# Batch 1 of x in one transfer of eight heads on the casting queue, instead of two of four

## The chip, the cores and the metric

The kernel runs on one core of one Trainium2 chip. The metric is device microseconds (us) of one execution; the three runs of the kernel before took 213.36, 213.55 and 213.91 us, median 213.55. The engines are named as the profile names them: PE (TensorE matmul), PEld (its weight loads), DVE (VectorE), ACT (ScalarE), POOL (GpSimd), SP (SyncE). Each has its own instruction stream, executed in order, and waits on semaphores that other engines and transfers raise.

## The reference

Two steps. The first is a cross attention in which, for each of 8 batches and 8 heads, 512 token rows `x` and 32 state rows `state` (64 wide) read each other with the same scores, the softmax taken over the state rows for the one and over the token rows for the other:

```python
scores = scale * np.matmul(x, state.transpose(0, 1, 3, 2))
a = np.exp(scores - scores.max(-1, keepdims=True))
a /= a.sum(-1, keepdims=True) + 1e-09
xread = np.matmul(a, state)                        # tokens read the state
scores2 = scale * np.matmul(state, x.transpose(0, 1, 3, 2))
a2 = np.exp(scores2 - scores2.max(-1, keepdims=True))
a2 /= a2.sum(-1, keepdims=True) + 1e-09
sread = np.matmul(a2, x)                           # the state reads the tokens
attn = np.concatenate([xread, sread], axis=2)      # 8 x 8 x (512 + 32) x 64
```

The second is a gated feed-forward layer over the 4352 rows of `attn` (8 heads side by side, 512 wide):

```python
gate = 1.0 / (1.0 + np.exp(-(x @ w_gate)))         # 512 -> 1536
out = gate * (x @ w_val) @ w_out                   # 1536 -> 512, float32
```

## The kernel before, in words

Nothing is scheduled by a planner: the instructions of each engine stand in the order in which the kernel's body calls its helpers, one flat list of calls from L563 on for the start and batches 0 to 2, then `step(b, f)` for the rest. The framework only adds the semaphore waits that the data need.

For a batch `b` the work goes: load x (tile `xf`, 128 partitions x 8 heads x 4 rows x 64), cast it to bfloat16, transpose it on PE into `xT`, multiply by the state (`Sp`), exponential on ACT (`E`), row sums and reciprocals on DVE (`rsq`, `riq`), normalize (`ab`), transpose on PE (`aTp`, copied to `aT`). The attention read is folded into the first layer: `state @ w` is formed once per batch (`swp`, copied to `SW`), and `gvp` = `SW` x `aT` gives gate and value at once. `rdp` is the read of the tokens by the state. The output product uses a seven-product scheme over halves of the matrices (`outp`).

The lines that the change touches belong to the first 14 us.

- **x of batch 0** comes as float32 in four transfers of two heads, all issued by SP (`load_xp`, L87), and is cast on ACT or DVE (`cast_xp`, L95). Its scores are done in quarters: `Sq_mm`, `Sq_exp`, `nq_sum`, `nq_mul`, one for each two heads.
- **x of batch 1** comes through the queue of POOL, which can cast on the way, so it lands as bfloat16 (`load_xh`, L100): heads 0 to 3 in one transfer, heads 4 to 7 in another. On the same queue stand, in order, the weights in pieces (`load_w`, L104) and the state (`load_sb`, L527). Every transfer on this queue gets the next of eight completion semaphores, DMASW0 to DMASW7, in turn; the one that comes ninth waits for the first, and so on.
- **PE** transposes heads 0 to 3 of batch 1 in `xT_mm(1, 0, S0, 2)` (8 transposes, L132) and heads 4 to 7 in `xT_mm(1, 2, S1, 2)`. Between the two stand on PE `Sq_mm(0, 3)` (scores of heads 6 and 7 of batch 0, L174) and `warm(3, G0)` (three matmuls on a tile of zeros, L517).

The calls in that piece, in the order of the list (`load_x...` and `nq_...` calls between them left out): `xT_mm(0, 3, S3)`, `xT_mm(1, 0, S0, 2)`, `Sq_mm(0, 3, OU)`, `warm(3, G0)`, `xT_mm(1, 2, S1, 2)`, `S_mm(1, 0, OU)`, `aT_mm(0, AT)`. On ACT: `xT_cp(0, 3)`, `Sq_exp(0, 1)`, `Sq_exp(0, 3)`, `xT_cp(1, 0)`, `S_exp(1, 0)`, `aT_cp(0, 0)`. On DVE: `nq_sum` of quarters 2, 0, 1, 3, then `nq_mul` of quarters 3 and 2, then `xT_cp(1, 2)`.

Of the kernel before, what the change touches and what calls it, by code (L numbers as in the profile page):

```python
# [16 lines left out]
def kernel(  # L17
# [71 lines left out]
    def xh_tile(b):  # L89
        if b not in xhs:  # L90
            xhs[b] = stg.tile((128, H, 4, D), BF, name="xf", padded_shape=(128, 2 * H, 4, D))

    def cast_xp(b, cp, lo, n):
        xh_tile(b)
        cp(xhs[b][:, lo:lo + n], xfs[b][:, lo:lo + n])  # L95

    def load_xh(b, lo, n):
        xh_tile(b)
        v = x[b].rearrange("h (p c) d -> p h c d", c=4)
        nc.gpsimd.dma_start(xhs[b][:, lo:lo + n], v[:, lo:lo + n])  # L100
# [9 lines left out]
    def zero(t, eng):  # L110
        (nc.gpsimd if eng is pool else nc.vector).memset(t, 0.0)
# [455 lines left out]
    zero(sbz, pool)  # L567
    warm(4, S1)
    make_identity(nc, ident)
    load_xh(1, 0, 4)  # L570
    nc.vector.memset(ones, 1.0)
    cast_s(0, vec)
    cast_xp(0, act, 0, 2)
    load_xh(1, 4, 4)
    zero(sTd, vec)
    sT_mm(0, S1)
    load_xp(0, nc.sync, 4, 2)
# [459 lines left out]
```

## Time and profile before

| | |
|---|---|
| runs | 213.36, 213.55, 213.91 us; median 213.55 |
| span of the profiled execution | 212.3 us, first to last instruction |
| median less that span | 1.25 us around it |
| PE busy | 204.3 us, 96% of the span |
| DVE, ACT, POOL busy | 76%, 61%, 37% |
| granted TensorE clock | 0.997 over the span |

The profile is of one execution. The page has the busy time of each engine, the span in 40 slices, and the chain of work that ended last: followed back from the last instruction, at each step to what released it. A row of the timeline reads: start, duration, engine, line, operation, output<-input, shape, count, and in brackets how long the engine sat idle before it and what released it. For a transfer, the last number is the time from its issue to its landing; a time window given with that view selects the issues that lie in it. The size of a transfer is that on the chip, so x of batch 1 counts 256 KB for four heads in bfloat16. In the rows of the DMA queues, q1 is the queue of SP, q10 that of ACT and q0 that of POOL.

### The profile page before, as it was taken

How to read it: one execution, taken by the hardware profiler on the slowest of the kernel's cores; microseconds unless marked ns; L12 is line 12 of the kernel's file. 1: busy time of each engine (PE TensorE's matmuls, PEld its weight loads, DVE VectorE, ACT ScalarE, POOL GpSimd, SP SyncE). 2: the span in 40 equal slices, each digit the busy share in tenths (PEclk: the TensorE clock that was granted, in tenths of full speed). 3: DMA queues.
4: the chain of work that ended last, by engine and by line, in shares of the span. 5: the costliest groups of instructions: out<-in, count | busy, mean ns of one | idle time of the engine just before them, and what ended most of it. 6: DMA issues, size and time to landing. Idle time of an engine off the chain costs nothing.

```text
span 212.3 us, 5333 instructions
## 1 busy us (share of the span) xinstructions
PE 204.3 (96%) x2089; PEld 132.9 (63%) x2089; DVE 160.3 (76%) x308; ACT 129.6 (61%) x244; POOL 78.1 (37%) x103
## 2 busy tenths in 40 slices
PE   7779999999999999999999999999999999999991
PEld 2545443677666666575666566657566666788981
DVE  2598899998987788578866887688748876865681
ACT  3878898754767477856786578647764663333210
POOL 8799458599042705900491029201500000000000
PEclk9999999999999999999999999999999999999998
DMA  6999999662589943996822621273110400221133
GB/s 205 163 192 191 214 289 183 119 212 40 78 224 333 136 91 110 302 94 208 249 42 48 173 99 28 58 120 153 29 31 35 166 2 0 99 102 49 39 112 99
DMA packets 41320, 27.14 MB, mean 128 GB/s; under 512 B 23632, under 2 KB 39248, under 8 KB 41296
## 3 DMA queue, kind: packets, MB, share of 16 engines
q1 hardware_dynamic: 31088, 20.00, 36.9%
q0 software_dynamic: 9776, 6.49, 19.8%
q10 hardware_dynamic: 432, 0.33, 0.6%
q8 instruction: 16, 0.26, 0.5%
q14 instruction: 8, 0.07, 0.1%
HBM read 18.35 MB, written 8.91 MB: 128 GB/s over the span
## 4 chain that ended last, share of the span: by engine, by line
PE 91%; DMA 3%; DVE 2%; ACT 1%; SPq 1%; issue 0%
PE gvp L355 30%; PE outp L425 29%; PE gvp L343 10%; PE gvp L358 5%; PE outp L442 4%; PE swp L286 4%; DMA xf<-in_x_dram 3%; PE swp L293 2%; PE outp L484 2%; PE Sp L147 1%; PE outp L467 1%; PE rdp L262 1%; SPq L87 1%; DVE rsq L186 1%; PE aTp L234 1%; PE rdp L265 1%
## 5 line engine op out<-in xcount | busy, mean ns | idle before, releaser
L369 DVE SCALAR_TENSOR_TENSOR glu<-th,gvp 128x512 bf16<-128x512 f32 (+1 forms) x108 | 70.1, 655 | 36.7 <-PE gvp L355 13.7
L364 ACT ACTIVATE th<-gvp 128x512 f32<-128x512 f32 (+1 forms) x108 | 62.1, 578 | 49.3 <-PE gvp L355 34.8
L355 PE MATMUL gvp<-aT,SW 128*128 128x512 bf16 x288 | 77.4, 379 | 0.1
L329 ACT CAST SW<-swp 128x512 bf16<-128x512 f32 x83 | 46.5, 592 | 9.3 <-PE swp L286 8.3
L425 PEld LDWEIGHTS <-Sm 128*128 128x128 bf16 x324 | 31.7, 98 | 12.6
L355 PEld LDWEIGHTS <-SW 128*128 128x128 bf16 x288 | 26.7, 98 | 17.3 <-issue 3.6
L200 POOL CAST Eb<-E 128x256 bf16<-128x256 f32 x32 | 12.8, 438 | 52.0 <-ACT E L167 52.0
L425 PE MATMUL outp<-tw,Sm 128*128 128x256 bf16 x240 | 31.8, 273 | 0.0
L425 PEld LDWEIGHTS <-glu 128*128 128x128 bf16 x240 | 23.5, 98 | 10.2
L425 PE MATMUL outp<-wo,glu 128*128 128x256 bf16 x168 | 22.9, 273 | 0.0
L343 PE MATMUL gvp<-aT,SW 128*128 128x512 bf16 x96 | 22.6, 379 | 0.0
L227 POOL TENSOR_TENSOR ab<-E,ri 128x512 bf16<-128x512 f32 x13 | 14.3, 1100 | 11.8 <-DVE ri L210 7.1
L407 DVE TENSOR_TENSOR Sm<-glu 128x768 bf16<-128x768 bf16 (+1 forms) x34 | 18.0, 535 | 0.0
L433 DVE SCALAR_TENSOR_TENSOR res<-outp,U 128x512 f32<-128x512 f32 x22 | 15.0, 685 | 1.2 <-PE outp L442 0.9
L343 PEld LDWEIGHTS <-SW 128*128 128x128 bf16 x96 | 8.6, 97 | 10.4 <-issue 1.8
L116 POOL CAST xb<-xf 128x1024 bf16<-128x1024 f32 x12 | 13.2, 1128 | 1.9 <-DMA xf<-in_x_dram 1.9
L358 PE MATMUL gvp<-xb,wgv 128*128 128x256 bf16 x96 | 12.6, 272 | 0.0
L167 ACT ACTIVATE E<-Sp 128x512 f32<-128x512 f32 x14 | 8.4, 599 | 6.7 <-PE Sp L147 5.7
L425 PE MATMUL outp<-wo,Sm 128*128 128x256 bf16 x84 | 11.5, 273 | 0.0
L358 PEld LDWEIGHTS <-wgv 128*128 128x128 bf16 x96 | 9.3, 98 | 1.3
L251 POOL CAST xs<-xf 128x1024 bf16<-128x1024 f32 x10 | 10.2, 1044 | 0.0
L425 PE MATMUL outp<-tw,glu 128*128 128x256 bf16 x72 | 9.8, 273 | 0.0
(105 smaller groups left out, 213.3 us busy)
## 6 DMA issues: line engine op xcount, KB each, us to landing
out_dram<-res SPq DMA_DIRECT2D x14, 512.0 KB, 3.4
xf<-in_x_dram SPq DMA_DIRECT2D x5, 1024.0 KB, 7.5
wo<-in_moe_w_out_dram POOLq DMA_DIRECT2D x3, 512.0 KB, 7.8
xf<-in_x_dram SPq DMA_DIRECT2D x4, 256.0 KB, 3.9
wgv<-in_moe_w_gate_dram POOLq DMA_DIRECT2D x4, 256.0 KB, 7.7
wgv<-in_moe_w_val_dram POOLq DMA_DIRECT2D x4, 256.0 KB, 8.8
xf<-in_x_dram POOLq DMA_DIRECT2D x1, 1024.0 KB, 9.5
out_dram<-res SPq DMA_DIRECT2D x3, 256.0 KB, 2.2
```

The source lines that it names most:

```text
L116: cp(xbs[b].rearrange("p c h d -> p h c d")[:, lo:lo + n], (xhs if b in xhs else xfs)[b][:, lo:lo + n])
L200: nc.gpsimd.tensor_copy(Ebs[b][:, c], E1s[b][:, c])
L227: (nc.gpsimd if eng is pool else nc.vector).tensor_tensor(half(b, i, abs_), e1, ri.unsqueeze(len(ri.shape)).to_broadcast(e1.shape), ALU.mult)
L329: cp(*sw_left.pop((b, lo, w, e)))
L343: nc.tensor.matmul(ps, SWs[b][:, g, w, fs], aTs[b][:, :, g], start=(g == 0), stop=(g == 1))
L355: nc.tensor.matmul(ps, SWs[b][:, g, w, fs], aTs[b][:, :, g], start=(g == 0), stop=(g == 1))
L358: nc.tensor.matmul(ps, (wg, wv)[w][:, j, fs], held["XS"][:, j], start=(j == 0), stop=(j == 3))
L364: nc.scalar.activation(th, held["gv", b, f][0], AF.Tanh, scale=0.5)
L369: nc.vector.scalar_tensor_tensor(glus[b][:, f], held["th", b, f], 1.0, held["gv", b, f][1], ALU.add, ALU.mult)
L407: eng.tensor_tensor(S_(b, t)[:, i], a, c, op)
L425: nc.tensor.matmul(wps[key][:, c], lhs[:, i, c * 128:(c + 1) * 128], rhs[:, i], start=(first and c == 0 and i == 0), stop=(i == NF // 2 - ...
L433: nc.vector.scalar_tensor_tensor(to, wps[key], 0.5, held["w", name], ALU.mult, ALU.add)
```

## The change

One call loads all eight heads at the place where the first four were loaded; the second call is gone.

```diff
     make_identity(nc, ident)
-    load_xh(1, 0, 4)
+    load_xh(1, 0, 8)
     nc.vector.memset(ones, 1.0)
     cast_s(0, vec)
     cast_xp(0, act, 0, 2)
-    load_xh(1, 4, 4)
     zero(sTd, vec)
```

On POOL, at the start of its list of transfers, two rows become one with twice the rows of data:

```order
 masks.py:199 ISA
 masks.py:199 AFFINE_SELECT ident<-ident 128x128 [waits Pool_49]
-L100 DMA xf<-in_x_dram 128x4x256 x2
+L100 DMA xf<-in_x_dram 128x8x256
 L104 DMA wgv<-in_moe_w_gate_dram 128x4x256
 L104 DMA wgv<-in_moe_w_val_dram 128x4x256
```

Everything behind it on POOL stands in the same order, and each transfer's completion semaphore has a number one lower.

On PE, at `xT_mm(1, 2, S1, 2)` (heads 4 to 7 of batch 1), the wait for the second transfer (DMASW1 before) falls away:

```order
 L517 LDWEIGHTS wm
 L517 MATMUL warm<-wm 128x512
-L132 LDWEIGHTS xf [waits DMASW1_49]
+L132 LDWEIGHTS xf
 L132 MATMUL xTp<-ident,xf 128x128 [waits PE_49]
 L132 LDWEIGHTS xf
```

Twenty-odd rows ahead of it on PE, where the last transpose of batch 0 (tile xf_133) is followed by the first of batch 1 (tile xf_128), the row that waits for DMASW0 stands as it did:

```order
L132 LDWEIGHTS xf_133
L132 MATMUL xTp_194<-ident_96,xf_133 128x128
L132 LDWEIGHTS xf_128 [waits DMASW0_49]
L132 MATMUL xTp_199<-ident_96,xf_128 128x128
L132 LDWEIGHTS xf_128
```

These are the rows of before; in the changed kernel the wait at this place has the same name, but DMASW0 is now raised by the transfer of all eight heads.

## Prediction

> **What bounds the kernel now.** I read the windows view first, because a share over the whole span mixes the start with the rest. Columns: stretch, its length, then busy time (and instructions) of PE, PEld, DVE, ACT and POOL, the granted clock, DMA share, GB/s.
>
> ```profile
> 2.00:8.40 6.40, 5.17 (x39) 2.37 (x36) 2.44 (x6) 3.51 (x7) 6.33 (x11) 1.00 1.01 240
> 8.40:14.00 5.60, 4.32 (x68) 2.79 (x72) 4.99 (x14) 4.39 (x10) 4.50 (x9) 1.00 1.41 187
> 14.00:205.00 191.00, 190.87 (x1960) 124.79 (x1960) 150.47 (x281) 120.86 (x229) 65.81 (x81) 1.00 0.55 124
> ```
>
> From 14 us to 205 us PE is busy for 190.87 of 191 us. So there is nothing in those 191 us that could take up a late start, and nothing that could be shortened by an earlier weight. Whatever moves the moment at which PE gets its backlog, at about 14 us, moves the end by the same amount. Before that PE has holes, and the chain of waits says what sets its pace there (start, length, what):
>
> ```profile
> 2.27 5.45 DMA xf<-in_x_dram
> ...
> 7.74 0.62 ACT xf L95
> 8.36 0.29 ACT E L182
> 8.65 0.03 issue
> 8.68 0.43 DVE rsq L186
> ...
> 10.41 0.29 DVE rsq L186
> ...
> 10.73 0.21 DVE riq L188
> ...
> 10.97 1.06 DVE ab L193 x2
> ...
> 12.17 0.62 PE aTp L234 x8
> ...
> 12.81 1.08 ACT aT L244 x2
> ...
> 13.94 0.42 PE rdp L265 x32
> ```
>
> The last transfer of x of batch 0 lands at 7.72, then ACT casts it, then four reductions and reciprocals follow each other on DVE, one for each quarter of batch 0. The fourth of them, at 10.41, is that of heads 6 and 7. After it come the normalization, the transposes of `ab`, the copies of `aT` and at 13.94 PE's unbroken work. The transfers of batch 1 do not stand in this chain. The question is how far from it they are. The timeline of that piece:
>
> ```profile
> 7.74 0.62 ACT L95 CAST xf<-xf 128x512 bf16<-128x512 f32 x1 [0.34 <-DMA xf<-in_x_dram]
> 8.41 0.23 PEld L132 LDWEIGHTS <-xf 128*128 128x128 bf16 x4 [0.55 <-ACT xf L95]
> 8.81 0.45 PEld L132 LDWEIGHTS <-xf 128*128 128x128 bf16 x8 [0.17 <-DMA xf<-in_x_dram]
> 8.85 0.59 ACT L135 COPY xT<-xTp 128x512 bf16<-128x512 bf16 x1
> 9.33 0.87 ACT L182 ACTIVATE E<-Sp 128x256 f32<-128x256 f32 x2
> 9.48 0.17 PEld L174 LDWEIGHTS <-xT 128*128 128x128 bf16 x4 [0.23 <-ACT xT L135]
> 9.59 0.34 PEld L517 LDWEIGHTS <-wm 128*128 128x128 bf16 x3
> 10.10 1.01 ACT L135 COPY xT<-xTp 128x1024 bf16<-128x1024 bf16 x1
> 10.37 0.45 PEld L132 LDWEIGHTS <-xf 128*128 128x128 bf16 x8 [0.43 <-DMA xf<-in_x_dram]
> ```
>
> The row at 8.81 is `xT_mm(1, 0)`, heads 0 to 3 of batch 1: PE already waits there, 0.17 us, for the first transfer. The row at 10.37 is `xT_mm(1, 2)`, heads 4 to 7: it waits 0.43 us for the second. Between them PE does the scores of heads 6 and 7 of batch 0 (9.48), which feed the second exponential in the ACT row at 9.33 (it ends at 10.20) and through it the fourth reduction of the chain.
>
> **The change part by part.**
>
> *One wait removed.* The wait of 0.43 us at 10.37 goes. Nothing in the chain comes from there: `aT_mm(0)` at 12.17 is released by `ab`, not by batch 1. Worth nothing.
>
> *One issue removed on POOL.* Two issues take 1.68 us together, a later one of eight heads in float32 takes 0.93:
>
> ```profile
> 2.73 1.68 POOL L100 DMA_DIRECT2D xf<-in_x_dram  x2
> 4.39 0.75 POOL L104 DMA_DIRECT2D wgv<-in_moe_w_gate_dram  x1
> 10.02 1.19 POOL L193 TENSOR_TENSOR ab<-E,riq 128x256 bf16<-128x256 f32 x2 [1.10 <-DVE riq L188]
> 11.96 1.42 POOL L200 CAST Eb<-E 128x256 bf16<-128x256 f32 x4
> 21.92 0.93 POOL L82 DMA_DIRECT2D xf<-in_x_dram  x1
> ```
>
> So the six transfers behind it are issued some 0.7 us sooner, and POOL waits longer ahead of its first `ab` at 10.02, where it has 1.10 us idle already. Their landing isn't set by the issue but by the queue, below, so this too is worth nothing. If the weights did come sooner, the PE row of the long window shows that no time is lost to them. If they came later by up to a microsecond, PE would be as late by then.
>
> *One transfer in place of two.* This is the part that costs. The semaphore that `xT_mm(1, 0)` waits for is now raised when all eight heads have landed. PE stands still at 8.81 until then; behind it on PE are the scores of heads 6 and 7, the `warm` matmuls, and all the rest. When does the merged transfer land? The issues, one window for each half and the next (time from issue to landing last), and the packets that the queue of POOL (q0) and of SP (q1) moved in the microseconds from 4 (q1 alone), 5, 6, 7 and 10:
>
> ```profile
> xf<-in_x_dram POOLq DMA_DIRECT2D x1, 256.0 KB, 6.0
> ...
> xf<-in_x_dram POOLq DMA_DIRECT2D x1, 256.0 KB, 6.7
> wgv<-in_moe_w_gate_dram POOLq DMA_DIRECT2D x1, 256.0 KB, 7.3
> ```
>
> ```profile
> q1 hardware_dynamic: 378, 0.36, 106.7%
> ...
> q0 software_dynamic: 155, 0.08, 60.2%
> q1 hardware_dynamic: 183, 0.17, 53.9%
> ...
> q0 software_dynamic: 280, 0.14, 103.3%
> ...
> q0 software_dynamic: 207, 0.10, 80.4%
> ...
> q0 software_dynamic: 394, 0.19, 145.0%
> ```
>
> The first half lands at 2.73 + 6.0 = 8.73, the second at about 10.35 (PE goes on at 10.37), the first piece of weights at 4.39 + 7.3 = 11.7. The steps are 1.6 and 1.35 us for equal sizes: the queue is a stream that works off its bytes in order. Merging doesn't lessen the bytes. Three values for the landing L:
>
> - If the stream's slowest engine is never idle today, L stays at 10.35.
> - If the 0.25 us by which the step between the halves exceeds the next step come from the second issue, they go: 8.73 + 1.35 = 10.1.
> - Lower end: all of the slack in the stream goes. Eight heads are 1024 packets of 512 B (0.51 MB); 155 move from 5 to 6 us beside the tail of batch 0 as today, the other 869 at the 394 per us of the full stream, 2.2 us, so until 8.2. Today the first half's 512th packet moves at 7.4 (155 + 280 by 7, then 77 of 207) and the landing is at 8.73, 1.3 later. That gives L = 9.5.
> - Upper end: no packet moves until all rows of the transfer are described, as late as the second issue ended today, 0.75 us after the first: 10.35 + 0.75 = 11.1.
>
> I take L = 10.2, between the first two, since both rest on the steps of the very rows.
>
> From L to the end: the eight weight loads start 0.05 us after it and take 0.45 us (the rows at 8.81 and 10.37), so the scores of heads 6 and 7 start at L + 0.52 instead of 9.48, a shift of L - 8.96. That step had waited 0.23 us for the ACT copy of `xT` anyway, which is why the shift is less than that of the wait. Their exponential now starts when the scores are done, the same shift, and ends at 10.20 + (L - 8.96). The fourth reduction started at 10.41 because DVE was busy with the third; with its exponential at 10.20 and 0.03 us of hand-over it had 0.18 us to spare. Chain shift: L - 8.96 - 0.18 = L - 9.14. With L = 10.2 that is **1.06 us**, and at 9.14 the cost would begin. The rest of the chain (0.21, 1.06, 0.62, 1.08 us) keeps its lengths. The transposes of heads 0 to 3 are copied on ACT behind the late exponential, then PE does `S_mm(1, 0)`; that follows the exponential's end by 1.0 us for the copy and ends before `aT_mm(0)` at about 13.2, so it adds nothing. POOL's `Eb` copies need the same exponential, which ends at about 11.4, before they start today (11.96).
>
> Sum: -0 (wait) -0 (issue) + 1.06 (PE held). The span of 212.3 becomes 213.4; with the 1.25 us by which the median of the runs exceeds that span, 214.6.
>
> **A rule that speaks for the change.** The Trainium skill, "DMA: Bandwidth & Descriptors", section "Anatomy of one DMA — SWDGE (gpsimd) path", gives a transfer a fixed cost of about 2.0 us and then bytes over 436 GB/s, and its rules for kernel authors say to coalesce. By it an estimate for the merged transfer is 2.0 + 2.4 us for the 1 MB read, after an issue that ends near 3.8: L = 8.2, no wait at all, and the time stays at 213.55. The trace does not agree for transfers that stand behind each other: steps of 1.35 us leave no room for 2.0 us each.
>
> **The rivals.**
>
> *Mostly hidden.* L is near its lower end, 9.5, because the two halves leave a hole: 207 packets from 7 to 8 us against 394 later. For it: that row. Against it: the last landing of a transfer is set by the slowest engine, and the halves' step of 1.6 us is only 0.25 over the later ones, so that engine hardly idles. Shift 0.36 us, 213.9: within what can be told from no change (0.3%, 0.64 us, which L = 9.78 would reach). This is also where the rule above would lead.
>
> *Late start.* L = 11.1, shift 1.96, 215.5. For it: q0 moved nothing before 5 us though its first issue ended at 3.66, so descriptions take time to become packets. Against: eight heads of float32 were issued in 0.93 us at 21.92, no more than 0.2 over a half.
>
> *Faster.* The last transfer of batch 0 shares the engines with q0 from 5 us on (183 packets of q1 beside 155). If the merged transfer starts moving later, batch 0 lands sooner; ACT, which had been idle for 0.34 us ahead of its cast at 7.74, starts the chain up to 0.34 us earlier: 213.2. It decides only if L is also below 9.14 - 0.34 = 8.8, and a transfer that starts later and still has all eight heads down by the time that four take today is hard to see.
>
> **How the numbers follow.** Forecast (L from 9.8 to 10.7) 0.63; mostly hidden 0.17; late start 0.15; faster 0.05. So slower 0.78, same 0.17, faster 0.05. The range 213.7 to 215.4 runs from L = 9.3 to L = 11.0; it leaves out the faster case, the tail of the hidden one and half of the late start.
>
> **What would show it.** Right: PE idle ahead of the `xT_mm(1, 0)` row rises from 0.17 to about 1.6 us with the transfer as releaser; that row starts at 10.2 to 10.3; the transfer's time to landing is about 7.5 us; `aTp` starts at about 13.2; the chain of waits goes from the transfer of batch 1 through the scores and exponential of heads 6 and 7 to the fourth reduction; from 15 us on each row is later by one constant. Wrong: the row starts before 9.2, or starts late while `aTp` still starts at 12.2 (something takes up the delay), or the delay at 14 us is gone by 205 us. The length of the steps after the landing would be wrong if the granted clock fell below 1.00 in this stretch.

## The result, and the profile after

The changed kernel takes 216.89 us (median of four runs, 216.12 to 217.54) against 213.73 for the kernel before in the same comparison (213.36 to 214.42): ratio 1.0127, 95% interval 1.0086 to 1.0169. A second comparison of the same code gave 216.58 against 213.72, ratio 1.0142 (1.0112 to 1.0173). (The quotient of the two medians, 1.0148, lies inside the first interval.) It is slower, as forecast, but by 2.7 to 3.2 us and not by 1.06: above the range of 213.7 to 215.4.

The windows of the changed kernel's profile, in 2 us steps where the pause lies (stretch, its length, busy time and instructions of PE, PEld, DVE, ACT, POOL, then the granted clock, DMA share, GB/s):

```profile
2.00:8.40 6.40, 5.11 (x43) 2.14 (x40) 3.38 (x7) 4.13 (x9) 6.17 (x10) 1.00 1.11 247
8.40:10.00 1.60, 0.00 (x0) 0.00 (x0) 1.21 (x5) 0.59 (x2) 0.72 (x2) 1.00 1.42 189
10.00:12.00 2.00, 0.21 (x3) 0.21 (x4) 0.00 (x0) 0.00 (x0) 1.22 (x2) 0.84 1.45 196
12.00:14.00 2.00, 2.00 (x15) 1.29 (x14) 0.47 (x2) 0.92 (x2) 0.47 (x2) 0.50 1.48 194
14.00:16.00 2.00, 1.99 (x31) 1.68 (x30) 1.80 (x5) 1.03 (x3) 2.00 (x4) 0.81 1.60 188
```

Two things stand here. PE does nothing from 8.4 to 11.8 (its last transposes, at 7.68 below, end at about 8.1), and DVE and ACT run dry at 10. And the granted clock, 1.00 throughout this stage before, goes to a half for about 3.4 us shortly before PE has work again. The timeline of the same profile, with the rows that answer to those of before:

```profile
7.01 0.62 ACT L95 CAST xf<-xf 128x512 bf16<-128x512 f32 x1
7.68 0.23 PEld L132 LDWEIGHTS <-xf 128*128 128x128 bf16 x4
9.04 0.40 DVE L186 TENSOR_REDUCE rsq<-E 128x8 f32<-128x256 f32 x1
11.79 0.77 PEld L132 LDWEIGHTS <-xf 128*128 128x128 bf16 x8 [3.88 <-DMA xf<-in_x_dram]
12.62 0.42 PE L174 MATMUL Sp<-tw,xT 128*128 128x64 bf16 x4
12.85 1.47 PE L517 MATMUL warm<-wm 128*128 128x512 bf16 x3
13.08 0.38 ACT L182 ACTIVATE E<-Sp 128x256 f32<-128x256 f32 x1 [4.09 <-PE Sp L174]
13.49 0.42 DVE L186 TENSOR_REDUCE rsq<-E 128x8 f32<-128x256 f32 x1 [3.81 <-ACT E L182]
13.53 1.87 POOL L200 CAST Eb<-E 128x256 bf16<-128x256 f32 x4 [2.31 <-ACT E L182]
14.18 0.96 DVE L193 TENSOR_TENSOR ab<-E,riq 128x256 bf16<-128x256 f32 x2
15.29 0.61 PE L234 MATMUL aTp<-ident,ab 128*128 128x128 bf16 x8
17.05 0.42 PE L265 MATMUL rdp<-xf,Eb 128*32 128x64 bf16 x32 [0.48 <-ACT aT L244]
```

PE waits 3.88 us for the transfer of eight heads, ACT 4.09 us behind it for the scores of heads 6 and 7, DVE 3.81 us for the exponential. The third reduction ran at 9.04, the fourth comes at 13.49. The three `warm` matmuls take 1.47 us; at full clock they took 0.81. `aTp` is 3.12 us later than before (15.29 for 12.17), `rdp` 3.11 (17.05 for 13.94). How long the transfer took to land, and the head of the chain of waits (start, length, what):

```profile
xf<-in_x_dram POOLq DMA_DIRECT2D x1, 512.0 KB, 9.0
```

```profile
2.73 9.02 DMA xf<-in_x_dram
...
11.79 1.04 PE xTp L132 x8
12.82 0.21 PE Sp L174 x4
13.04 1.28 PE warm L517 x3
14.32 0.72 PE xTp L132 x8
15.04 0.25 PE Sp L156 x8
...
15.31 0.60 ACT E L167
...
15.93 1.08 ACT aT L244 x2
```

The landing is 2.73 + 9.0 = 11.7. From there the chain runs over PE itself, the `warm` matmuls at half clock among it, then the batch 1 scores, their exponential on ACT and the copies of `aT` behind it on the same engine. Further on one more wait is new in this profile. PE in the changed kernel's timeline:

```profile
30.21 0.41 PE L286 MATMUL swp<-wgv,tw 64*32 64x512 bf16 x8
32.17 0.63 PE L286 MATMUL swp<-wgv,tw 64*32 64x512 bf16 x16 [0.24 <-DMA wgv<-in_moe_w_val_dram]
210.62 0.83 PE L467 MATMUL outp<-tw,glu 128*128 128x128 bf16 x12
```

and in that of before, the same three places (the second is one row with the eight matmuls ahead of it):

```profile
27.18 0.41 PE L286 MATMUL swp<-wgv,tw 64*32 64x512 bf16 x8
28.49 0.84 PE L286 MATMUL swp<-wgv,tw 64*32 64x512 bf16 x24
207.15 0.83 PE L467 MATMUL outp<-tw,glu 128*128 128x128 bf16 x12
```

The shift is 3.03 us at the first and 3.47 at the last. In between the value weights' columns 512 to 1023 make PE wait: 0.24 us of idle time stand ahead of the row at 32.17, and the rows behind it are later by 3.47. The spans differ by 3.5 (215.8 for 212.3). Nothing else comes or goes behind that.

### The profile page after: what moved, and what is told of

It is laid out like the page before. It is cut to its first block, busy times and chain, and to the rows that moved or that the text cites. A ratio compares the mean times of both kernels' runs of the same rounds, so it can differ in the third digit from the quotient of the medians.

```text
span 215.8 us, 5332 instructions
## 1 busy us (share of the span) xinstructions
PE 204.9 (95%) x2089; PEld 133.0 (62%) x2089; DVE 161.1 (75%) x308; ACT 129.6 (60%) x244; POOL 77.9 (36%) x102
## 4 chain that ended last, share of the span: by engine, by line
PE 84%; DMA 9%; POOL 2%; issue 1%; ACT 1%; DVE 0%; POOLq 0%
PE gvp L355 29%; PE outp L425 28%; DMA wgv<-in_moe_w_val_dram 5%; PE gvp L343 5%; PE gvp L358 5%; PE outp L442 4%; DMA xf<-in_x_dram 4%; PE swp L286 3%; PE outp L484 2%; PE swp L293 1%; PE Sp L147 1%; PE outp L467 1%; PE rdp L262 1%; PE xTp L132 1%; POOL wgv L104 1%
## 5 line engine op out<-in xcount | busy, mean ns | idle before, releaser
L200 POOL CAST Eb<-E 128x256 bf16<-128x256 f32 x32 | 13.2, 450 | 54.3 <-ACT E L167 52.0
L425 PEld LDWEIGHTS <-glu 128*128 128x128 bf16 x240 | 23.5, 98 | 10.2
L343 PEld LDWEIGHTS <-SW 128*128 128x128 bf16 x96 | 8.6, 98 | 10.5 <-issue 1.9
L116 POOL CAST xb<-xf 128x1024 bf16<-128x1024 f32 x12 | 13.2, 1127 | 2.4 <-DMA xf<-in_x_dram 2.4
L251 POOL CAST xs<-xf 128x1024 bf16<-128x1024 f32 x10 | 10.1, 1039 | 0.0
(105 smaller groups left out, 214.6 us busy)
## 6 DMA issues: line engine op xcount, KB each, us to landing
wgv<-in_moe_w_val_dram POOLq DMA_DIRECT2D x4, 256.0 KB, 10.5
```

What stands on the lines that cost most here:

```text
L116: cp(xbs[b].rearrange("p c h d -> p h c d")[:, lo:lo + n], (xhs if b in xhs else xfs)[b][:, lo:lo + n])
L200: nc.gpsimd.tensor_copy(Ebs[b][:, c], E1s[b][:, c])
L343: nc.tensor.matmul(ps, SWs[b][:, g, w, fs], aTs[b][:, :, g], start=(g == 0), stop=(g == 1))
L425: nc.tensor.matmul(wps[key][:, c], lhs[:, i, c * 128:(c + 1) * 128], rhs[:, i], start=(first and c == 0 and i == 0), stop=(i == NF // 2 - ...
```

## Experiments

The theory after the result: PE is held until all eight heads are down, and what stands behind the wait on PE (scores of heads 6 and 7) is on the chain; the landing is later than I took it; and the pause costs clock. The first rival: merging slows the queue itself. The second: the clock costs nothing, since ACT and DVE set the pace there.

### The wait's place on PE

```diff
-    xT_mm(1, 0, S0, 2)
     nq_sum(0, 2)
...
     warm(3, G0)
+    xT_mm(1, 0, S0, 2)
```

With one transfer:

> One transfer of eight heads, as in the change; on PE the scores of heads 6 and 7 of batch 0 and the three warm matmuls now stand ahead of the transposes that wait for it. Theory (PE is held at the wait and what is queued behind it is late, and the pause lowers the clock): the scores are free at about 8.7 us and the fourth reduction follows the third without a hole, but aT_mm(0) still stands behind the batch 1 transposes and their copy, so it starts at max(12.2, L + 2.0) for a landing L: with L near 11.7 at 13.7 instead of 15.3; PE pauses from about 9.5 to L, under 2.5 us, and the clock stays at 1.00. Time about 215.0, between before (213.7) and the change (216.9). Rival (the merged transfer slows the queue itself, so that everything behind it is late whatever PE does): no better than 216.5.

With two:

> The kernel before, two transfers of four heads, with the same move on PE alone. Theory: the first half lands at about 8.7, as PE gets there, so the move changes nothing by itself: 213.7 within 0.4. This is the other half of the comparison for the run with one transfer.

Measured: with one transfer a median of 214.9 us in four runs (a fifth, at 218.07, stands apart and is left out), ratio 1.0052 (1.0033 to 1.0071) to the kernel before at 213.81; with two 213.79, ratio 1.003 (0.9998 to 1.0062). As the theory has it: with only the place of one call changed, the same transfer costs 1.1 us (214.9 - 213.8) instead of 2.7 to 3.2. The rows with one transfer:

```profile
8.67 0.17 PEld L174 LDWEIGHTS <-xT 128*128 128x128 bf16 x4 [0.85 <-ACT xT L135]
10.79 1.31 PEld L132 LDWEIGHTS <-xf 128*128 128x128 bf16 x16 [1.68 <-DMA xf<-in_x_dram]
13.04 1.04 PE L234 MATMUL aTp<-ident,ab 128*128 128x128 bf16 x8
```

The scores of heads 6 and 7 run at 8.67; PE waits behind them, and `aTp` comes 2.25 us after PE goes on, not 3.5. One part of my expectation missed: the clock fell here too (0.990 over the span), after a wait of only 1.68 us.

### The wait without the merging

```diff
-    load_xh(1, 0, 4)
+    load_xh(1, 4, 4)
...
-    load_xh(1, 4, 4)
+    load_xh(1, 0, 4)
```

> The kernel before with its two transfers of batch 1 in the other order: heads 4 to 7 first. The first transposes of batch 1 then wait for the second transfer, with nothing merged. Theory (what counts is that PE waits for the last byte of batch 1): the wait ends where the merged transfer's would, 10.3 to 11.8, PE is held 1.5 to 3 us, and the time is 214.8 to 217, like the change. Rival (merging makes the landing itself late): the second transfer lands at 10.35 as before, the time is at most 214.9, and the change at 216.9 stays two us above it.

Measured: 216.55 us, ratio 1.0127 (1.0106 to 1.0148), the same as the change. So nothing has to be merged for a loss of this size; a wait of PE for the last byte is enough. That the two losses are equal looks like chance: the profile gets there by another way, and the expected landing of 10.3 to 11.8 was missed:

```profile
9.90 0.45 PEld L132 LDWEIGHTS <-xf 128*128 128x128 bf16 x8 [1.88 <-DMA xf<-in_x_dram]
11.33 1.43 POOL L200 CAST Eb<-E 128x256 bf16<-128x256 f32 x4
11.78 1.59 DVE L193 TENSOR_TENSOR ab<-E,riq 128x256 bf16<-128x256 f32 x2
13.52 0.61 PE L234 MATMUL aTp<-ident,ab 128*128 128x128 bf16 x8 [1.10 <-DVE ab L193]
```

```profile
11.90:15.32 3.42, 1.69 (x36) 1.27 (x40) 3.39 (x6) 1.81 (x5) 1.86 (x5) 1.00 1.57 190
15.32:18.73 3.41, 3.41 (x60) 1.43 (x67) 2.08 (x7) 2.43 (x5) 3.41 (x5) 0.50 1.44 197
```

The second half lands at 9.86 here, 1.9 us sooner than the eight heads in the change, so PE is held for less. But DVE's two products take 1.59 us instead of 1.06 beside POOL's `Eb` copies, which now run at the same time, and the clock falls later, from 15.32, when PE has no idle time left to lose. `aTp` is 1.7 us later than in the second profile of before (11.85, below), the span 2.9 (214.8 for 211.9): the other 1.2 falls behind `aTp`, where the one thing new is the stretch at half clock. So this run shows what the wait can cost, and not that a merged transfer lands as soon as the second of two; that is taken up below.

To see whether the `Eb` copies are what slows the product, they were moved behind the next issue on POOL, still with the halves swapped:

```diff
-    at_Eb(0)
...
     load_w(0, 1280, 256)
+    at_Eb(0)
```

> The two transfers in the other order (heads 4 to 7 first), and on POOL the four Eb copies of batch 0 moved behind the next issue of a weight, 0.74 us later. In the swapped run the two normalizing products on DVE took 1.59 us beside the Eb copies instead of 1.06 ahead of them. Theory (those copies and DVE's product slow each other): the DVE pair at line 193 falls to 1.0 to 1.2 us, aTp starts at L + 3.1 instead of L + 3.66, time 0.3 to 0.6 us under the swapped kernel's 216.5, unless the clock falls elsewhere. Rival (the pair is slow for another reason): 1.6 us again and the same time within 0.3.

Measured: 216.0 us, ratio 1.0113 (1.0075 to 1.0151). Over the kernel before that ran beside it this is 2.28 us, for 2.74 with the halves swapped alone: 0.46 less, within what these runs scatter. The product's row falls to 0.96 us, with the copies now behind its start:

```profile
12.48 0.96 DVE L193 TENSOR_TENSOR ab<-E,riq 128x256 bf16<-128x256 f32 x2
12.72 1.66 POOL L200 CAST Eb<-E 128x256 bf16<-128x256 f32 x4
```

The pair's time is as the theory said; that the 0.46 us come from it isn't shown, since the clock fell in this run at another time too (`aTp` came 3.5 us after PE went on, in a stretch of half clock). The Trainium skill, "SBUF — State Buffer", section "Who interferes with whom", says that DVE with two SBUF inputs and a GpSimd operation that reads SBUF exclude each other, and that the one that starts first blocks the other. The rows agree with the first half: wherever the two overlap one of them is slow, the products (1.59, with copies of 1.43) or the copies (1.66, with products of 0.96). They do not bear out the second half by the order in which the rows start: in the change, above, the copies start at 13.53, 0.65 us ahead of the products, and it is the copies that are slow (1.87) while the products take 0.96. What decides which of the two waits stays open.

### The same two kernels again

> The changed kernel once more, unchanged, for a second profile of the same code: does the transfer of eight heads land at 11.7 again, and does the clock fall again? In the two other undisturbed profiles of one transfer of eight heads so far known it landed at 10.75 (scores first) and 11.74 (the changed kernel). Theory (the landing is set by the slowest of 16 shares, which varies; a pause of PE of 2 us or more ahead of 12 us always costs the clock): landing between 9.8 and 11.8, one stretch of half clock of 3.4 us, 216 to 217.5. Rival (11.7 is what merging gives): 11.7 within 0.2.

> The kernel before once more, unchanged, for a second profile: in the one on record the last transfer of batch 0 landed at 7.72, in every profile of another kernel since at 6.4 to 6.6. If the 7.72 was one late share, the chain starts 0.7 us sooner here, the fourth reduction near 9.6 and aTp near 11.5, with the span near 211.9 and the time 213.7 within 0.4; the second half of batch 1 lands at 9.8 to 10.4.

> The changed kernel a third time, for one more landing: 10.6 to 11.8 by theory (slowest of 16 shares, later than the second half's 9.9 to 10.3 in five profiles of two transfers), with one or more stretches of half clock.

The changed kernel again: 216.58, `aTp` at 14.66, span 215.0, landing 2.73 + 8.4 = 11.1. A third time, one execution: 215.59 against 213.88, `aTp` at 13.32, span 213.8, landing at 9.66, with the clock at half for 6.8 us (8.8 to 15.6). So 11.7 is not what merging gives, and the rival in that expectation falls; but the third landing lies under the 10.6 that the theory gave as its lower end. The kernel before again: 213.83, span 211.9, and `aTp` at 11.85 for 12.17 on record:

```profile
11.85 0.61 PE L234 MATMUL aTp<-ident,ab 128*128 128x128 bf16 x8 [0.59 <-DVE ab L193]
```

The last transfer of batch 0 was late there too (the ACT cast starts at 7.43, at 6.9 to 7.3 in most others), against my expectation that the 7.72 on record was a stray: it comes and goes.

### The clock's part

```diff
+    warm(12, G0)
     xT_mm(1, 0, S0, 2)
```

> The change with twelve more matmuls on the zero tile (128x512, 0.215 us each at full clock, 2.6 us in all) ahead of the transposes that wait, so that PE's pause is at most about 1.2 us. It leaves all waits as they are. Theory (part of the loss is the clock): the granted clock stays at 1.00 from 5 us on, the chain shifts by L - 9.1 alone, and the time is about 0.5 to 0.9 us under the change, near 216.2. Rival (the clock costs nothing here since ACT and DVE set the pace until 16 us): the same as the change within 0.3.

> The change with twelve matmuls on the zero tile ahead of the transposes that wait, again, since the profiled run of the first try had the clock at half from end to end while its other runs took 215.6. Theory (1.0 to 1.3 of the 3 us are the clock): clock 1.00 from 5 us on, PE's pause under 1.5 us, aTp at L + 3.0 to 3.4, time 215.6 within 0.4, at least 0.8 under the change on the same chip. Rival: within 0.4 of the change.

and with eight instead of twelve:

> The change with eight matmuls on the zero tile ahead of the transposes that wait, not twelve: they end at about 9.7, before any landing of eight heads seen so far, so PE's start is set by the landing and not by them, and the 3.4 us stretch around the pause stays busy for over 2 us. Theory: the clock stays at 1.00; aTp starts 3.2 us after PE goes on; the time is 213.7 plus (L + 3.2 - 11.85), so 214.8 for L = 9.8, 216.1 for 11.1, 216.8 for 11.7; it tells how much of the change's 216.7 is landing and how much (0.3 by the two profiles so far) is clock. Rival (most of the loss is the clock, and the late landings were chance): 215.0 or less in most runs.

Measured with twelve: 215.61, ratio 1.0088 (1.0071 to 1.0105), and again 215.32, ratio 1.008 (1.0065 to 1.0095); the profiled execution of the first took 429 us with every matmul at half pace, and since its profile lists no granted clock under 1.00 it doesn't tell why. With eight: 215.51, ratio 1.0076 (1.0051 to 1.0101). All are 1.0 to 1.6 us under the change, and in the comparison that had the change and the twelve side by side the intervals do not meet (1.0112 and up, 1.0095 and down): work that does nothing, put in front of the wait, makes the kernel faster. The rows with twelve (second run), then two of the timeline with eight:

```profile
7.91 2.75 PE L517 MATMUL warm<-wm 128*128 128x512 bf16 x12
10.29 0.65 PEld L132 LDWEIGHTS <-xf 128*128 128x128 bf16 x8
13.48 0.61 PE L234 MATMUL aTp<-ident,ab 128*128 128x128 bf16 x8 [0.46 <-DVE ab L193]
```

```profile
11.60 0.45 PEld L132 LDWEIGHTS <-xf 128*128 128x128 bf16 x8 [2.22 <-DMA xf<-in_x_dram]
14.59 0.61 PE L234 MATMUL aTp<-ident,ab 128*128 128x128 bf16 x8 [0.46 <-DVE ab L193]
```

and the window with eight in which the matmuls stand:

```profile
8.10:11.52 3.42, 1.78 (x9) 0.59 (x6) 1.55 (x6) 0.96 (x3) 2.08 (x4) 1.00 1.42 189
```

With eight the landing was at 11.56 in the profiled run, the clock stayed full, and `aTp` came 14.59 - 11.56 = 3.03 us after it. That is the prediction's own step: 12.17 + (L - 9.14) is L + 3.03. In the first two profiles of the change `aTp` came 15.29 - 11.74 = 3.55 and 14.66 - 11.10 = 3.56 after the landing, in the third 13.32 - 9.66 = 3.66. So the clock costs 0.5 to 0.6 us up to `aTp` there, and the rival that it costs nothing falls. In the third the half clock goes on behind `aTp`, and from there to `rdp` it takes 2.21 us instead of 1.77: 0.4 more, so 1.1 in all, beside 0.8 for the landing (9.66 + 3.03 - 11.85). My expectation of 1.0 to 1.3 holds for that profile alone. With twelve, the matmuls themselves set PE's start: the transfer had landed at 9.77, PE went on at 10.29 and 10.5, and `aTp` came 3.7 us after the landing. There `aTp` is 1.63 us behind the second profile of before, and the span 1.6 (213.5 for 211.9): the delay of `aTp` goes to the end whole.

In the profiled executions the eight gain 1.1 us on the change (216.40 for 217.54): 0.2 by the landing, 0.5 by the clock up to `aTp`, and 0.4 because PE does not wait for the value weights. Where the rest of the gain in the medians comes from isn't shown. The landings were at 9.8, 9.8 and 11.6 for 11.7, 11.1 and 9.7; with three of each that may be chance.

### The start reordered

```diff
-    xT_mm(1, 0, S0, 2)
...
-    warm(3, G0)
+    warm(8, G0)
+    xT_mm(1, 0, S0, 2)
...
+    aT_mm(0, AT)
+    aT_cp(0, 0, act)
+    aT_cp(0, 1, act)
     S_mm(1, 0, OU)
     S_exp(1, 0)
...
-    aT_mm(0, AT)
-    aT_cp(0, 0, act)
...
-    aT_cp(0, 1, act)
```

With one transfer, then with two:

> One transfer of eight heads, with the start reordered: scores of heads 6 and 7 and eight zero matmuls ahead of the batch 1 transposes, the transposes and copies of ab of batch 0 ahead of the batch 1 scores on PE and ACT. Theory (the transfer costs by what stands behind its wait): batch 0's chain depends on the landing only by max(11.6, L + 1.1), so for L = 10 to 10.7 aTp starts at 11.6 to 11.9 and the time is 213.3 to 214.2; for L = 11.7 it is 214.9. Rival (the late batch 1 itself costs, whatever stands in front): 215 or more.

> The same reordered start with the two transfers of four heads. Theory: aTp at 11.5 to 11.7, time 213.3 to 213.8; no more than 0.5 under the run with one transfer.

Measured: 215.02, ratio 1.006 (1.0039 to 1.0082), and 215.81, ratio 1.0092 (1.0052 to 1.0131). Neither beats the kernel before, so both forecasts of the time missed. `aTp` did come at 12.02 with one transfer, but then DVE held PE up, which has its row sums of batch 1 ahead of the copy of `SW` that PE needs:

```profile
PE gvp L343 <- DVE SW L329: 0.6, 1, 0.6
PE swp L293 <- DMA wgv<-in_moe_w_val_dram: 0.4, 1, 0.4
```

The chain of waits shows where that comes from. The copies of `aT`, moved forward, now stand on ACT ahead of the exponential of batch 1, which starts at 13.77 (11.60 before), and the row sums wait for it:

```profile
12.79 0.98 ACT aT L244 x2
13.77 0.51 ACT E L167
...
14.30 0.70 DVE rs L208
```

The kernel with two transfers lost the clock in its profile and waited more in the same place (1.0 us). Among its six runs the three with a mean clock of 0.997 or more took 214.79 to 215.02; the six such runs with one transfer took 214.66 to 215.23. So at full clock one transfer and two take the same in this order, as the theory had it (no more than 0.5 apart), and the order itself loses about 1.1 us with either. The rival, that a late batch 1 costs whatever stands in front, has its number (215 or more) but isn't shown: here PE comes to batch 1 late with two transfers as well, behind eight matmuls that end at 11.07 in the one profile and, at half clock, at 12.70 in the other. No run of this study shows a kernel faster than the one before.

### Why the landing varies

A transfer's completion semaphore is raised 16 times in these traces; the landing is the last of the 16, and a share here is what stands behind one of them. The time to landing of one transfer of eight heads, issued at 2.73 each time, in the eight profiles in which the weights follow at once: 6.9, 7.0, 7.1, 8.0, 8.3, 8.4, 8.8 and 9.0 us. The second of two halves, issued at 3.66, in six: 6.2, 6.4, 6.4, 6.4, 6.5 and 6.7. The same last byte lands at 9.9 to 10.3 with two transfers, and at 9.7 to 11.7 with one: three of the eight sooner than all six, five later than all six. So one transfer spreads the landing; that it is later on the whole, these fourteen don't show.

The stream isn't slower, so the rival that merging slows the queue itself finds no support. The middle of the 16 shares lands at 8.7 to 9.4 with two transfers and at 8.8 to 9.5 with one. What differs is the end: in the change 15 shares were down by 9.81 and the last at 11.74. In five of the eight the last share came 0.9 to 2.0 us behind the fourteenth, in one of the six second halves (1.1; 0.3 to 0.7 in the others). To see whether the weights behind it on the queue do that, a memset of 3.5 us on POOL was put between them:

```diff
     load_xh(1, 0, 8)
+    nc.gpsimd.memset(Sm.rearrange("p t i n -> p (t i n)")[:, :4096], 0.0)
```

> The change with a memset of 4096 columns on POOL (about 3.7 us, into a tile that is not used until much later) between the transfer of eight heads and the first piece of weights, so that for some 3.5 us nothing stands behind that transfer on its queue. It leaves nothing out; the time itself is of no interest, as all weights come later. Theory (the late share of a transfer is late because the other shares go on to the weights at once and take the bandwidth, where with two transfers a hole of a third of the rate lets it catch up): the landing is 9.3 to 9.9 with no share more than 0.6 us behind the others. Rival (some shares lose a microsecond now and then whatever else moves): the landing is again anywhere from 9.7 to 11.7.

> The same kernel as the run with the POOL gap, for a second landing: theory 9.3 to 9.9, rival anywhere from 9.7 to 11.7.

> The same kernel as the run with the POOL gap, for a third landing: theory 9.3 to 9.9, rival anywhere from 9.7 to 11.7.

> The same kernel as the run with the POOL gap, for a fourth landing: theory 9.3 to 9.9, rival anywhere from 9.7 to 11.7. Of the eight profiles of one transfer without the gap five landed later than 10.7, so four out of four under 10 would be chance about once in fifty.

The four took 6.7, 6.6, 6.5 and 6.8 us to land, so 9.2 to 9.5, all as the theory said. (Their times, 216.4 to 217.0, say nothing, since all weights come later.) But the memset did something else as well. DVE in the first of them:

```profile
3.59 3.89 DVE L532 CAST sb<-sf 128x256 bf16<-128x256 f32 x1 [2.65 <-DMA sf<-in_state_dram]
7.54 0.48 DVE L111 MEMSET tw<- 128x512 uint32 x1
```

A cast that took 0.29 us in the second profile of before (0.60 in the change) takes 3.89 and ends 0.15 us behind POOL's memset (3.80 to 7.33). DVE stood still in all that time. So the queue was emptied and DVE was stopped at once. In two runs the queue was empty and DVE free, the six transfers moved behind POOL's first product:

```diff
-    load_w(0, 256, 256)
-    load_w(1, 256, 256)
-    load_w(0, 1024, 256)
-    load_w(1, 1024, 256)
-    load_sb(2)
-    load_w(1, 0, 256)
...
     nq_mul(0, 0, pool)
+    (the six, in the same order)
```

> The change with the six transfers that follow the eight heads on POOL moved behind POOL's first product of batch 0 (about 9.9 us), and no memset. In the four runs with the memset the landing was 9.2 to 9.5, but DVE also stood still from 3.6 to 7.5 us: its cast took 3.89 us beside the memset instead of 0.29. Here POOL is idle instead, so DVE works as in the change. Theory (the weights behind it on the queue keep a late share late): landing 9.2 to 9.7 again. Rival (what helped was that DVE was still): anywhere from 9.7 to 11.7.

> The same kernel as the run with the late weights, for a second landing: theory 9.2 to 9.7, rival anywhere from 9.7 to 11.7.

7.7 and 7.4 us, so 10.4 and 10.1 (the times, 218.7 and 220.0, again hold the late weights): neither as early as the theory said nor as late as the worst. With nothing behind them on the queue the last two or three shares still came about a microsecond behind the rest (9.74 and 10.43 for 9.19 or sooner; 9.97 to 10.13 for 8.99 or sooner). The weights on the queue are therefore not the whole of it. What makes a share late, and whether DVE's work in that time has a part in it, stays open.

## Why the prediction was right and wrong

- **"From 14 us to 205 us PE is busy ... moves the end by the same amount": right.** With the clock full (twelve matmuls) 1.63 us at `aTp` were 1.6 in the span. In the change 3.12 at `aTp` became 3.5 in the span; it grows from 3.03 to 3.47 at the wait for weights at 32.17.
- **"The wait of 0.43 us at 10.37 goes ... Worth nothing" and "One issue removed on POOL ... worth nothing": right in sum.** The issue took 1.08 us, and the next started at 3.80 instead of 4.39. No weight was wanted sooner.
- **"If they came later by up to a microsecond, PE would be as late by then": wrong in one place.** Before, the value weights landed at 18.07 + 10.4 = 28.5, and the row at 28.49 used them: there was no slack to lend. In the change they were issued at 21.06, 2.99 us later and so no later than PE, but took 11.1 us to land, and PE waited at 32.17. In the second profile they took 10.3 and PE did not wait there, so this price too comes and goes.
- **"Chain shift: L - 8.96 - 0.18 = L - 9.14": right.** At full clock with the landing at 11.56 (eight matmuls) the formula gives `aTp` at 14.59, and that is what was measured. It is one profile.
- **"I take L = 10.2": the step that failed.** The landing in the profiled execution was 11.74, beyond the upper end of 11.1 as well. That end was put down to a late start. That isn't what happened: the middle shares were as early as with two transfers, and it was the last one or two of 16 that were late, in five of eight profiles by 0.9 to 2.0 us. The argument for the first bound, that the slowest share sets the landing and is never idle, took the slowest share of one profile for that of all. Why a share comes late stays open. With L = 11.74 the same formula gives 2.60 of the 3.12 us at `aTp`. Had L been 9.7, as in the third profile, the sum would have come out too low all the same, by the next step.
- **The clock was given no price: the other step that failed.** The last line of the prediction named it as what would make the steps wrong, and neither the sum nor a rival had it. It costs 0.5 us up to `aTp` in the change, 1.1 in all in its third profile and, in the swapped kernel, 1.2 behind `aTp`. PE's idle time was forecast at 1.6 us, and 1.68 was enough to lose the clock with the scores first.
- **"with the 1.25 us by which the median of the runs exceeds that span": a third term that was too small.** Where an execution's time and its own span are both known, they differ by 1.7 to 1.8 us (217.54 for 215.8 in the change, 213.69 for 211.9 in the second profile of before). By that (an estimate, since the time of that one execution isn't on record) the profile of before was of an execution about 0.5 us slower than the median. Part of that is its last transfer of batch 0, which landed late: in the second profile `aTp` stood at 11.85, and there the cost begins at L = 8.82, not 9.14.
- **The four together.** From 214.6 to the 217.54 of the profiled execution there are 2.9 us: 1.54 of landing (11.74 for 10.2), 0.52 of clock up to `aTp`, 0.4 of growth behind `aTp`, and 0.5 of the 1.25.
- **The rivals.** *Mostly hidden* did not happen: the earliest landing without a gap, 9.7, still went with 215.59; 1.1 us of its loss is the clock. *Late start* was nearest in size. Something of it is there: from 5 to 6 us the queue of POOL moved 82 and 75 packets in the first two profiles of the change, 155 and 157 in the two of before. But 15 of the 16 shares were down at 9.81 in the first of them, so the start isn't what set the landing there. *Faster*: batch 0 did land sooner in the change (the cast at 7.01 for 7.74), and it gained nothing, as argued; but with two transfers too the cast starts anywhere from 7.1 to 7.8, so this isn't shown to come from the merging. *The rule for coalescing* gave a landing of 8.2; no run came under 9.2, and the estimate by the Trainium skill, "DMA: Bandwidth & Descriptors", section "Anatomy of one DMA — SWDGE (gpsimd) path", was short by 1 to 3.5 us in this place.
- **"What would show it".** PE idle 3.88 us instead of 1.6, the start at 11.79 instead of 10.2 to 10.3, 9.0 us to landing instead of 7.5, `aTp` at 15.29 instead of 13.2; the chain goes through the transfer of batch 1, but then over PE and the exponential of batch 1 rather than through DVE's fourth reduction, since PE at half clock had become the later of the two.

## What to carry to other kernels

A transfer is worth splitting where its first part feeds something that stands ahead of critical work on an in-order engine: what the merged transfer costs is set by what is queued behind its wait, and two transfers in the wrong order can cost as much. Where the landing of a transfer is a term of a sum, one profile's landing is one draw: take its spread over the other transfers of the same queue, on the late side above all. And a pause added to PE should be priced twice, once as delay and once as a stretch of 3.4 us at half clock, whose cost depends on whether PE is full when it comes. A profile's span is best set beside the time of its own execution: where that lies off the median, so does every slack read from it.

## What the runs showed of the hardware that was not expected

**The clock falls without an idle stretch.** It falls and rises in pieces of 3.4 us. What PE did in the piece before a fall, by the windows view: 0.14 and 0.32 us busy in two profiles of the change, but also 1.55 with the scores first, 1.69 with the halves swapped (its row stands above), 1.84, 1.89 and 2.03 in three others. These two are of scores first and of the third profile of the change:

```profile
7.77:11.18 3.41, 1.55 (x18) 0.77 (x16) 3.15 (x10) 1.52 (x5) 2.46 (x5) 1.00 1.35 176
```

```profile
5.39:8.81 3.42, 2.03 (x32) 1.31 (x28) 1.98 (x6) 3.18 (x7) 3.04 (x5) 1.00 1.36 187
```

It did not fall after 1.78 us in the run with eight matmuls of 512 columns, nor after 1.83 in the swapped run, nor after 2.02 and 2.10 in two others. So half of a piece is about where it turns here; from 1.78 to 2.03 both are seen, so the busy time of this view alone doesn't decide. At half clock a piece with PE busy for 2.51 us was followed by another at half (third profile of the change), one with 2.98 (the change) and one with 3.17 (scores first) by full clock. The Trainium skill, "TensorE: Matmul & The Clock Gate", section "What's actually happening", gives the same 3.4 us, free-running, and says that the clock falls after an idle window; the length agrees, the "idle" doesn't: pieces with PE busy for half their time were enough.

**POOL's memset stops DVE.** The cast of 0.29 us took 3.73 to 3.89 beside it in all four runs (above). The Trainium skill, "SBUF — State Buffer", section "Who interferes with whom", tells of a lock held for a whole instruction, and the end of the cast 0.15 us behind the memset agrees. By the rows the cast started 0.21 us ahead of the memset (3.59 for 3.80), while POOL was still issuing the transfer, and waited all the same.
